# Third column block of an expert's first layer computed at 448 columns ahead of the branch, and the last tile's scaled copy in two halves

## The chip, the cores and the metric

The kernel runs on one core of a Trainium2 chip. A core has five engines with queues of their own: PE (TensorE, matrix products), ACT (ScalarE), DVE (VectorE), POOL (GpSimd) and SP (SyncE, which here only issues transfers). The metric is the device time of one execution in microseconds (us), and the median of the runs counts.

## What is computed

An attention layer with random features is followed by a mixture of experts with 8 experts, on 4 x 576 = 2304 tokens of 512 features. The part that the change touches is the second one:

```python
expert_idx = np.argmax(x @ w_gate, axis=1)              # one expert per token
# disp[e, 0:counts[e]] = rows of x that chose e, at most capacity = 576
h = np.maximum(np.einsum('ecd,edf->ecf', disp, w1), 0.0)     # D 512 -> F 1024
y = np.einsum('ecf,efd->ecd', h, w2)                         # F 1024 -> D 512
out[i] = gate_w[i] * y[expert_idx[i], pos[i]]
```

All inputs are float32. The kernel keeps that precision by splitting each operand into a high and a low part and adding three products: high x high, low x high, high x low.

## The kernel before

**Stages.** The first 165 us or so hold the attention and the routing, which scatters the rows of each expert into a DRAM buffer. Then `opening()` works on the expert that led after the first rows, and a loop takes `e` = 1 to 7. Each expert is one pass: `between(e - 1)` prepares it (transposes its first two tiles of 128 rows, splits the first five blocks of `w1`, finishes the last tile of the expert before, computes the block f = 0 of the first layer at columns 0 to 256), and then `expert(e)` runs.

**Tiles and blocks.** Rows of an expert are columns of the first layer's product: `xh` and `xl` (high and low part) hold up to 576 of them, in tiles of 128. `wide` is 256 columns, `most` is 448. The 1024 hidden features are 8 blocks `f` of 128. `ffn1(f, bank, o, o2, at)` computes block f for the columns o to o2 into PSUM bank `ph` number `bank`, from column `at` on: 4 times L812 (high weights x `xh`) and L813 (low weights x `xh`) in turn, then 4 times L815 (high weights x `xl`), so 12 matmuls. `relu` (L826 on ACT, then L829 on DVE) turns a bank into `h` and its low part.

**Branches.** `expert(e)` asks how many rows the expert has. With over 256 it takes the arm `many`: `prep` transposes tiles 2 and 3 on PE (L745, 4 for each tile), ACT copies each into `xh` (L746) and DVE makes `xl` (L747); PE goes on with f = 1 and f = 2 at 256 columns, for which tiles 0 and 1 suffice. Then a second branch: over 448 rows `to_all`, else `to_most`, which adds the columns 256 to 448 of f = 0, 1 and 2 and does f = 3 to 7 at 448 columns at once. After each `relu`, `behind` splits the next weight block (L117 on ACT, L123 on DVE) and `loads` has SP fetch the next expert's rows and weights (f = 0 and f = 2). Then `later` does the second layer for the tiles 1 to 3; tile 0 is done in the next `between`, or, for the last expert, in the two last lines of the kernel.

**Order.** Each engine takes its instructions in the order in which the code above writes them (a manual schedule), and waits on semaphores where it needs another engine's result. A wait on one engine's semaphore is a count: it covers everything that this engine did up to there.

**The end.** `put` scales a finished tile of the second layer with the gate (`y = py * gt`, L858 on ACT, from a PSUM bank) and has POOL scatter it to the output (L169). For the very last tile `py` is the bank `sm` and `e` is 7.

Of the kernel before, what the change touches and what calls it, by code (L numbers as in the profile page):

```python
# [14 lines left out]
AF = mybir.ActivationFunctionType  # L15
ALU = mybir.AluOpType
# [8 lines left out]
NE, DM, DFF = 8, H * D, 1024  # L25
# [12 lines left out]
def tile_kernel(ctx: ExitStack, tc: tile.TileContext, qT, kT, vT, vv, w_phi, w_g, w1, w2, out, cap):  # L38
    nc = tc.nc
# [128 lines left out]
    def to_out(rows, idx):  # L168
        dma = nc.gpsimd.indirect_dma_start(  # L169
            out=out, out_offset=bass.IndirectOffsetOnAxis(ap=idx.bitcast(U32), axis=0),  # L170
            in_=rows, in_offset=None, bounds_check=NT - 1, oob_is_err=False)
        tc.declare_no_dep(dma.ins, group="outs", reason="distinct rows")
        tc.add_to_no_dep_group("outs", dma.ins)
# [550 lines left out]
    wide = 2 * P  # L724
    most = wide + 3 * D
# [15 lines left out]
    def prep(e, s0, m, pt=None):  # L741
        pt = pt_t[s0 // P % 2] if pt is None else pt
        xh, xl = x2_l[0][:, :, 0], x2_l[0][:, :, 1]
        for k in range(4):
            nc.tensor.transpose(pt[:, k, 0:m], xi_t[e % 2, s0][0:m, k * P:(k + 1) * P], ident[0:m, 0:m])  # L745
        nc.scalar.activation(xh[:, :, s0:s0 + m], pt[:, :, 0:m], AF.Copy)  # L746
        nc.vector.tensor_tensor(xl[:, :, s0:s0 + m], pt[:, :, 0:m], xh[:, :, s0:s0 + m].bitcast(F32),  # L747
                                ALU.subtract)
# [58 lines left out]
    def ffn1(f, bank, o, o2, at=0):  # L807
        hi, lo = w_t[f // 4]
        fs = slice((f % 4) * P, (f % 4 + 1) * P)
        acc = ph_t[bank][:, at:at + o2 - o]  # L810
        for k in range(4):
            nc.tensor.matmul(acc, hi[:, k, fs], xh[:, k, o:o2], start=(k == 0), stop=False)  # L812
            nc.tensor.matmul(acc, lo[:, k, fs], xh[:, k, o:o2], start=False, stop=False)  # L813
        for k in range(4):
            nc.tensor.matmul(acc, hi[:, k, fs], xl[:, k, o:o2], start=False, stop=(k == 3))  # L815
# [8 lines left out]
    def relu(f, bank, o, o2):  # L824
        cuts = sorted({o, o2, *(x for x in [o2 - few(o2)] if o < x < o2)})
        nc.scalar.activation(h_t[f][:, o:o2], ph_t[bank][:, 0:o2 - o], AF.Relu)  # L826
        for a, b in zip(cuts, cuts[1:]):
            at = rest_at(o2, a)
            beat[0] = nc.vector.scalar_tensor_tensor(h_t[f][:, at:at + b - a], ph_t[bank][:, a - o:b - o], 0.0,  # L829
                                           h_t[f][:, a:b].bitcast(F32), ALU.max, ALU.subtract)  # L830
# [18 lines left out]
    def put(e, s0, m, bank):  # L849
        gt, it = gi_t[e % 2, s0]  # L850
        py, y = py_t[bank], y_t[bank % 2]
        if m <= D:
            half = half_t[bank % 2]
            nc.vector.tensor_copy(half[0:m], py[m:2 * m])
            nc.vector.tensor_tensor(half[0:m], half[0:m], py[0:m], ALU.add)
            nc.scalar.activation(y[0:m], half[0:m], AF.Copy, scale=gt[0:m])
        else:
            nc.scalar.activation(y[0:m], py[0:m], AF.Copy, scale=gt[0:m])  # L858
        to_out(y[0:m], it[0:m])


    def between(e):
        t = tiles[0 if e else 2]
        ffn2(wide, *t, 0, range(5))
        prep_gi(e + 1)
        for f in range(2):
            w_split(0, f)
        for x in tiles[:2]:
            prep(e + 1, *x)
        for f in range(2, 5):  # L870
            w_split(f // 4, f % 4)
        ffn2(wide, *t, 0, range(5, 8))
        put(e, *t, 0)
        ffn1(0, 0, 0, wide)
# [8 lines left out]
    def loads(e, f):  # L883
        if f in (0, 2) and e + 1 < NE:
            ask(e + 1, f // 2)

    def later(e, todo, n):
        for i, t in enumerate(todo):
            bank = 3 - i % 2 if len(todo) % 2 else 2 + i % 2
            ffn2(n, *t, bank)  # L890
            put(e, *t, bank)

    def cut(n, t0=1):
        return [(s0, min(m, n - s0)) for s0, m in tiles[t0:] if s0 < n]

    def w2_split(e, *fs):
        for f in fs:
            w_split(2 + f // 4, f % 4)
            if f % 4 == 3 and e + 1 < NE:
                w_load(e + 1, 2 + f // 4)  # L900

    def behind(e, f):
        if f < 3:
            w_split(1, f + 1)
        else:
            w2_split(e, f - 3)

    def to_most(e):
        for f in range(8):
            if f < 3:  # L910
                ffn1(f, f % 4, wide, most, at=wide)
            else:
                ffn1(f, f % 4, 0, most)
            relu(f, f % 4, 0, most)
            behind(e, f)
            loads(e, f)
        w2_split(e, 5, 6, 7)
        later(e, cut(most), most)

    def to_all(e):  # L920
        for f in range(8):
            if f >= 3:
                ffn1(f, f % 4, 0, wide)
            relu(f, f % 4, 0, wide)
            behind(e, f)
            loads(e, f)
            if f == 2:
                for t in tiles[4:]:
                    prep(e, *t)
        w2_split(e, 5, 6, 7)  # L930
        for f in range(8):
            ffn1(f, f % 4, wide, slots)
            relu(f, f % 4, wide, slots)
        later(e, cut(slots), slots)

    def to_two(e):
        for f in range(8):
            if f >= 3:
                ffn1(f, f % 4, 0, wide)
            relu(f, f % 4, 0, wide)  # L940
            behind(e, f)
            loads(e, f)
        w2_split(e, 5, 6, 7)
        later(e, cut(wide), wide)

    def to_one(e):
        for f in range(3):
            relu(f, f % 4, 0, P)
            behind(e, f)
            loads(e, f)  # L950
        for f in range(3, 9):
            if f < 8:
                thin1(f)
                thin_sum(f)
            if f > 3:
                thin_relu(f - 1)
            if f in (4, 6, 7):
                w2_split(e, (f - 3) // 2)
        w2_split(e, *range(3, 8))

    def expert(e):
        with tc.If(cv[e] > wide, label=f"many{e}") as many:
            told(f"most{e}", cv[e] > most)
            for t in tiles[2:4]:
                prep(e, *t)
            for f in range(1, 3):
                ffn1(f, f % 4, 0, wide)
            with tc.If(cv[e] > most, label=f"most{e}") as full:
                to_all(e)
            with full.Else():  # L970
                to_most(e)
        with many.Else():
            told(f"two{e}", cv[e] > P)
            for f in range(1, 3):
                ffn1(f, f % 4, 0, wide)
            with tc.If(cv[e] > P, label=f"two{e}") as two:
                to_two(e)
            with two.Else():
                to_one(e)
# [3 lines left out]
    def told(label, goes):  # L983
        tc.mark_branch_hint_location(label, hint=goes, engines=engines[:3])
# [24 lines left out]
    def opening():  # L1009
# [20 lines left out]
        prep_gi(0, 0, 1)  # L1030
        ffn2(wide, *tiles[0], 1)
        put(0, *tiles[0], 1)
        with tc.If(few_seen > wide - 1, label="seen") as enough:
            ffn2(wide, *tiles[1], 0, range(5))
# [29 lines left out]
    for e in range(NE):  # L1064
        if e:
            if e + 1 < NE:
                count(e + 1)
            expert(e)
        if e == 0:
            nc.vector.tensor_tensor(zi_t, tokf, drop_t, ALU.subtract)  # L1070
        elif e + 1 < NE:
            for b in range(3 * e - 3, 3 * e):
                to_out(fill[:, 0:DM], zi_t[:, b:b + 1])
        if e + 1 < NE:
            told(f"many{e + 1}", cv[e + 1] > wide)
            between(e)
# [35 lines left out]
```

## Time and profile before

| | |
|---|---|
| device time, median of 3 runs (lowest to highest) | 426.77 us (425.67 to 428.6) |
| device time of the profiled execution | 428.85 us |
| its span, first to last instruction | 427.1 us |
| mean granted TensorE clock | 0.989 |
| PE busy / ACT busy / DVE busy | 95% / 58% / 62% |
| passes `e` = 6 and `e` = 7, the two that take `to_most` | from 332.15 to about 374.5, and to about 417 |

All times in a trace are us from the start of the span. A view of the timeline gives each instruction's start and duration; PE's durations overlap, since matmuls are pipelined, so what a matmul costs a busy PE is the distance from start to start. The chain of waits (the chain that ended last) gives that distance directly: each of its pieces is the time that one step added. "<-" names what ended a wait.

### The profile page before, as it was taken

The page shows a single profiled execution, that of the slowest core. Times are in us where ns is not written, and L with a number is a line of the kernel's source. Part 1 is how long each engine was busy: PE and PEld are TensorE (multiplying, and loading weights), DVE is VectorE, ACT ScalarE, POOL GpSimd, SP SyncE. Part 2 cuts the span into 40 slices and gives each one's busy share as a digit, 9 for nine tenths or more (in the row PEclk, how much of TensorE's full clock was granted, in tenths as well). Part 3 has the DMA queues.
Part 4 walks back from the last instruction along what each step waited for, and adds up shares of the span by engine and source line. Part 5 has one row for each costly group of instructions (what it writes and reads, how often), then busy time and mean ns, then how long its engine had stood idle before and what let it go on. Part 6 is the DMA issues. An engine that isn't in the chain of part 4 may idle for free.

```text
span 427.1 us, 12167 instructions
## 1 busy us (share of the span) xinstructions
PE 407.4 (95%) x4813; PEld 358.0 (84%) x4813; DVE 264.7 (62%) x585; ACT 245.9 (58%) x452; POOL 175.1 (41%) x215
## 2 busy tenths in 40 slices
PE   5999999979999999999999999999999999999992
PEld 4778888868898788979979898989898998799871
DVE  5776897858787787744237984757475465156410
ACT  2988687688775586713137865656465454155410
POOL 1758566457576598740035205133250500160011
PEclk9999999998999999999999999999999999999997
DMA  7990599379606653479005996786949266210010
GB/s 250 387 350 5 181 344 357 120 262 296 204 4 214 203 187 122 155 263 363 11 31 171 355 347 213 278 275 176 361 163 331 102 233 216 109 35 1 2 51 29
DMA packets 42715, 82.78 MB, mean 194 GB/s; under 512 B 4351, under 2 KB 9343, under 8 KB 42624
## 3 DMA queue, kind: packets, MB, share of 16 engines
q1 hardware_dynamic: 38080, 72.13, 50.4%
q0 software_dynamic: 4544, 9.47, 6.1%
q8 instruction: 53, 0.87, 0.9%
q14 instruction: 38, 0.31, 0.2%
HBM read 62.65 MB, written 24.30 MB: 204 GB/s over the span
## 4 chain that ended last, share of the span: by engine, by line
PE 91%; DVE 3%; POOL 1%; issue 1%; DMA 1%; ACT 1%; POOLq 0%; SPq 0%; ACTq 0%; DVEq 0%
PE acc L341 10%; PE ph L812 9%; PE ph L813 9%; PE ph L815 9%; PE acc L370 8%; PE pr L259 4%; PE sm L845 4%; PE sm L843 4%; PE sm L846 4%; PE ph L843 4%; PE ph L845 4%; PE ph L846 4%; PE pt L355 4%; PE pr L260 3%; PE pt L745 2%; PE pr L254 1%
## 5 line engine op out<-in xcount | busy, mean ns | idle before, releaser
L169 POOL DMA_INDIRECT out<-y,it x22 | 24.7, 1122 | 165.4 <-ACT y L858 86.8
L123 DVE TENSOR_TENSOR l<-raw,h 128x512 fp32r<-128x512 f32 x118 | 80.1, 710 | 19.7 <-ACT h L117 16.6
L195 POOL TENSOR_TENSOR stk<-px,stk 64x1024 f16<-64x1024 f32 (+1 forms) x30 | 70.9, 2362 | 39.7 <-ACT stk L194 38.8
L812 PE MATMUL ph<-xh,h 128*128 128x256 f32 (+3 forms) x292 | 79.4, 298 | 0.2 <-issue 0.2
L813 PE MATMUL ph<-xh,l 128*128 128x256 f32 (+3 forms) x292 | 78.9, 296 | 0.0
L117 ACT ACTIVATE h<-raw 128x512 fp32r<-128x512 f32 x128 | 75.9, 630 | 0.0
L826 ACT ACTIVATE h<-ph 128x256 fp32r<-128x256 f32 (+3 forms) x67 | 28.8, 430 | 52.9 <-PE ph L815 51.2
L829 DVE SCALAR_TENSOR_TENSOR h<-ph,h 128x256 fp32r<-128x256 f32 (+2 forms) x91 | 33.2, 387 | 38.8 <-ACT h L826 37.9
L812 PEld LDWEIGHTS ph<-xh,h 128*128 128x128 f32 x292 | 55.6, 190 | 1.6 <-issue 0.4
L265 DVE TENSOR_REDUCE m<-pr 128x4 f32<-128x512 f32 x72 | 49.3, 684 | 11.8 <-PE pr L260 7.1
L813 PEld LDWEIGHTS ph<-xh,l 128*128 128x128 f32 x292 | 55.7, 191 | 0.9
L269 DVE TENSOR_TENSOR d<-pr,m 128x512 f32<-128x512 f32 x72 | 49.7, 690 | 3.5
L815 PE MATMUL ph<-xh,h 128*128 128x256 f32 (+3 forms) x292 | 50.9, 296 | 0.0
L341 PE MATMUL acc<-v,kp 128*64 128x73 f32 (+1 forms) x1280 | 47.0, 232 | 1.7 <-issue 1.7
L341 PEld LDWEIGHTS acc<-v,kp 128*64 128x64 f32 (+1 forms) x1280 | 41.2, 138 | 6.6 <-issue 2.7
L370 PE MATMUL acc<-kv,qp 128*64 128x73 f32 x1152 | 44.8, 229 | 0.4 <-issue 0.4
L370 PEld LDWEIGHTS acc<-kv,qp 128*64 128x64 f32 x1152 | 39.3, 136 | 6.5 <-issue 6.2
L815 PEld LDWEIGHTS ph<-xh,h 128*128 128x128 f32 x292 | 42.7, 191 | 0.6
L259 PE MATMUL pr<-whi,stk 128*128 128x128 f16 x260 | 37.0, 222 | 3.3 <-POOL xr L411 3.0
L260 PE MATMUL pr<-wlo,stk 128*128 128x128 f16 x260 | 36.5, 220 | 0.2 <-issue 0.2
L357 ACT ACTIVATE qp<-pt 128x512 f32<-128x512 f32 x36 | 21.5, 597 | 23.9 <-PE pt L355 23.8
L194 ACT ACTIVATE stk<-px 64x1024 f16<-64x1024 f32 (+1 forms) x30 | 34.5, 1150 | 1.0 <-DMA px<-in_kT 0.5
(163 smaller groups left out, 712.5 us busy)
## 6 DMA issues: line engine op xcount, KB each, us to landing
raw<-in_w SPq DMA_DIRECT2D x28, 1024.0 KB, 7.9
xs<-fill SPq DMA_DIRECT2D x18, 514.0 KB, 6.4
xr<-xs SPq DMA_DIRECT2D x24, 257.0 KB, 8.2
raw<-in_w SPq DMA_DIRECT2D x8, 512.0 KB, 3.8
vt<-in_vT SPq DMA_DIRECT2D x3, 1152.0 KB
v<-in_vv SPq DMA_DIRECT2D x2, 1314.0 KB, 7.4
px<-in_kT SPq DMA_DIRECT2D x5, 512.0 KB, 8.9
px<-in_qT SPq DMA_DIRECT2D x4, 640.0 KB, 12.8
```

Source lines behind the costliest of these rows:

```text
L117: nc.scalar.activation(hi, a, AF.Copy)
L123: engine.tensor_tensor(lo, a, hi.bitcast(F32), ALU.subtract)
L195: return lambda: nc.gpsimd.tensor_tensor(t[other], x, t[own], ALU.subtract)
L259: nc.tensor.matmul(pr[:, j], lt, whi, start=True, stop=False)
L260: nc.tensor.matmul(pr[:, j], lt, wlo, start=False, stop=True)
L265: nc.vector.tensor_reduce(m.rearrange("p a b -> p (a b)"), pr, AX.X, ALU.max, apply_absolute_value=True)
L269: beat[0] = nc.vector.tensor_tensor(d, pr, m.to_broadcast([P, 4, NF]), ALU.subtract)
L341: nc.tensor.matmul(acc[f:f + D, a, j * GC:(j + 1) * GC], kp[lo:hi, j, a, f:f + D], vt[lo:hi, r, h * GC:(h + 1) * GC], start=first and j == ...
L370: nc.tensor.matmul(num[lo:hi, g, j * GC:(j + 1) * GC], qp[:, a, j, lo:hi], kv_t[b][:, a, 4 * g + j], start=(a == 0), stop=(a == 1))
L812: nc.tensor.matmul(acc, hi[:, k, fs], xh[:, k, o:o2], start=(k == 0), stop=False)
L813: nc.tensor.matmul(acc, lo[:, k, fs], xh[:, k, o:o2], start=False, stop=False)
L815: nc.tensor.matmul(acc, hi[:, k, fs], xl[:, k, o:o2], start=False, stop=(k == 3))
```

## The change

Two edits. In the arm `many`, f = 2 is computed at 448 columns ahead of the second branch, in place of 256; `to_most` then adds columns 256 to 448 for f = 0 and f = 1 alone. (`to_all`, which starts again from column 256, is written as before; no expert of this input takes it.) In `put`, the last tile of the last expert is scaled in two halves of 256 columns, the first by ACT, the second by DVE.

```diff
-            nc.scalar.activation(y[0:m], py[0:m], AF.Copy, scale=gt[0:m])
+            c = DM // 2 if e == NE - 1 and not s0 else DM
+            nc.scalar.activation(y[0:m, 0:c], py[0:m, 0:c], AF.Copy, scale=gt[0:m])
+            if c < DM:
+                nc.vector.tensor_scalar(y[0:m, c:DM], py[0:m, c:DM], gt[0:m], None, ALU.mult)
         to_out(y[0:m], it[0:m])
...
     def to_most(e):
         for f in range(8):
-            if f < 3:
+            if f < 2:
                 ffn1(f, f % 4, wide, most, at=wide)
-            else:
+            elif f > 2:
                 ffn1(f, f % 4, 0, most)
             relu(f, f % 4, 0, most)
...
             for t in tiles[2:4]:
                 prep(e, *t)
-            for f in range(1, 3):
-                ffn1(f, f % 4, 0, wide)
+            ffn1(1, 1, 0, wide)
+            ffn1(2, 2, 0, most)
             with tc.If(cv[e] > most, label=f"most{e}") as full:
```

PE in the arm `many` of `e` = 7, from the end of f = 1 (bank `ph_3481`) into f = 2 (bank `ph_3482`), before:

```order
L815 MATMUL ph_3481<-xh_2709,h0_2705 128x256 x4
L812 MATMUL ph_3482<-xh_2709,h0_2705 128x256 [waits Activation_49]
L813 MATMUL ph_3482<-xh_2709,l0_2706 128x256 [waits DVE_49]
L812 MATMUL ph_3482<-xh_2709,h0_2705 128x256
L813 MATMUL ph_3482<-xh_2709,l0_2706 128x256
```

The same place and, behind the alternating rows, the end of f = 2 with the branch, of the change (the first and last rows of the block):

```order
L815 MATMUL ph_3481<-xh_2709,h0_2705 128x256 x4
L812 MATMUL ph_3482<-xh_2709,h0_2705 128x448 [waits Activation_49]
L813 MATMUL ph_3482<-xh_2709,l0_2706 128x448 [waits DVE_49]
L812 MATMUL ph_3482<-xh_2709,h0_2705 128x448
L813 MATMUL ph_3482<-xh_2709,l0_2706 128x448
L812 MATMUL ph_3482<-xh_2709,h0_2705 128x448
L813 MATMUL ph_3482<-xh_2709,l0_2706 128x448
L812 MATMUL ph_3482<-xh_2709,h0_2705 128x448
L813 MATMUL ph_3482<-xh_2709,l0_2706 128x448
L815 MATMUL ph_3482<-xh_2709,h0_2705 128x448 [waits DVE_49]
L815 MATMUL ph_3482<-xh_2709,h0_2705 128x448 x3
L971 COMPARE_AND_BRANCH
```

The 12 matmuls of f = 2 now read 448 columns, so tiles 2 and 3 as well; their first one waits for ACT, and the first L815 has a wait for DVE that it did not have.

PE in `to_most` of `e` = 7, where f = 1's second piece ends, before:

```order
L815 MATMUL ph_3481<-xh_2709,h0_2705 128x192 x4
L812 MATMUL ph_3482<-xh_2709,h0_2705 128x192
L813 MATMUL ph_3482<-xh_2709,l0_2706 128x192
L812 MATMUL ph_3482<-xh_2709,h0_2705 128x192
L813 MATMUL ph_3482<-xh_2709,l0_2706 128x192
```

And of the change:

```order
L815 MATMUL ph_3481<-xh_2709,h0_2705 128x192 x4
L812 MATMUL ph_3483<-xh_2709,h0_2705 128x448
L813 MATMUL ph_3483<-xh_2709,l0_2706 128x448
L812 MATMUL ph_3483<-xh_2709,h0_2705 128x448
L813 MATMUL ph_3483<-xh_2709,l0_2706 128x448
```

The 12 matmuls of f = 2's second piece are gone, and f = 3 (bank `ph_3483`) follows f = 1's at once.

DVE at the end of the program, before:

```order
L804 SCALAR_TENSOR_TENSOR h_3447<-sum_3479,h_3447 128x128 [waits Activation_49]
L123 TENSOR_TENSOR l2_3449<-raw_2890,h2_3448 128x512 [waits Activation_49]
L123 TENSOR_TENSOR l3_3451<-raw_3095,h3_3450 128x512 [waits DMAHW4_49,Activation_49]
L123 TENSOR_TENSOR l3_3451<-raw_3095,h3_3450 128x512 [waits Activation_49] x3
L976 UNCONDITIONAL_BRANCH
L1108 UNCONDITIONAL_BRANCH
```

And of the change:

```order
L123 TENSOR_TENSOR l3_3451<-raw_3095,h3_3450 128x512 [waits DMAHW4_49,Activation_49]
L123 TENSOR_TENSOR l3_3451<-raw_3095,h3_3450 128x512 [waits Activation_49] x3
L979 UNCONDITIONAL_BRANCH
L861 TENSOR_SCALAR y_3472<-sm_132,gt_3462 128x256 [waits DMASW1_49,DMASW6_49,DMASW0_49,Activation_49]
L1111 UNCONDITIONAL_BRANCH
```

DVE got one instruction, the second half of the last tile, and this one waits for ACT and not for PE, although PE writes the bank `sm` that it reads.

POOL at the end of the program, before:

```order
L976 ISA [waits DMASW7_49]
L962 ISA [waits DMASW2_49,DMASW1_49,DMASW0_49]
L976 UNCONDITIONAL_BRANCH
L169 DMA out_0<-y_3472,it_3463 2304x512 [waits DMASW3_49,Activation_49,Pool_49]
L1108 UNCONDITIONAL_BRANCH
```

And of the change:

```order
L979 ISA [waits DMASW7_49]
L965 ISA [waits DMASW2_49,DMASW1_49,DMASW0_49]
L979 UNCONDITIONAL_BRANCH
L169 DMA out_0<-y_3472,it_3463 2304x512 [waits DMASW3_49,DVE_49,Pool_49]
L1111 UNCONDITIONAL_BRANCH
```

The last scatter waited for ACT's copy; it now waits for DVE's half, and no longer for ACT by itself.

## Rows read from the trace of the kernel before

**Rows 1.** The page: shares of the span in the chain that ended last.

```profile
PE 91%; DVE 3%; POOL 1%; issue 1%; DMA 1%; ACT 1%; POOLq 0%; SPq 0%; ACTq 0%; DVEq 0%
```

**Rows 2.** Busy time by stretch: length, then PE, PEld, DVE, ACT, POOL, clock, DMA.

```profile
340.27:344.27 4.00, 4.00 (x38) 4.00 (x37) 1.95 (x6) 2.13 (x4) 0.00 (x0) 1.00 0.03 9
344.27:356.46 12.19, 12.19 (x62) 11.30 (x61) 7.00 (x16) 5.32 (x10) 0.00 (x0) 1.00 0.78 268
```

**Rows 3.** Chain in e = 6: start, us added. First L812 of six groups of 12.

```profile
338.83 0.12 PE ph L812
...
340.27 0.09 PE ph L812
...
341.59 0.11 PE ph L812
...
342.93 0.11 PE ph L812
...
346.73 0.20 PE ph L812
...
349.16 0.20 PE ph L812
```

**Rows 4.** Groups by line and shape: count, busy us, mean ns, idle before.

```profile
L812 PE MATMUL ph<-xh,h 128*128 128x256 f32 x196 | 49.6, 285 | 0.2 <-issue 0.2
...
L812 PE MATMUL ph<-xh,h 128*128 128x448 f32 x40 | 14.6, 366 | 0.0
...
L812 PE MATMUL ph<-xh,h 128*128 128x192 f32 x24 | 5.6, 271 | 0.0
```

**Rows 5.** Timeline of e = 6: transposes, ACT's and DVE's copies, f = 2's first matmul.

```profile
336.37 1.03 PE L745 MATMUL pt<-ident,xr 128*128 128x128 f32 x8
...
337.00 1.09 ACT L746 ACTIVATE xh<-pt 128x512 fp32r<-128x512 f32 x2 [1.05 <-PE pt L745]
...
337.63 1.29 DVE L747 TENSOR_TENSOR xh<-pt,xh 128x512 fp32r<-128x512 f32 x2 [1.23 <-ACT xh L746]
...
338.67 0.28 PE L812 MATMUL ph<-xh,h 128*128 128x256 f32 x1
```

**Rows 6.** The same four of e = 7.

```profile
378.69 1.04 PE L745 MATMUL pt<-ident,xr 128*128 128x128 f32 x8
...
380.37 1.09 ACT L746 ACTIVATE xh<-pt 128x512 fp32r<-128x512 f32 x2 [2.10 <-PE pt L745]
...
381.00 0.69 DVE L747 TENSOR_TENSOR xh<-pt,xh 128x512 fp32r<-128x512 f32 x1 [2.27 <-ACT xh L746]
381.00 0.28 PE L812 MATMUL ph<-xh,h 128*128 128x256 f32 x1
```

**Rows 7.** Timeline of e = 6: relu of f = 0, SP's load; then ACT's first split for e = 7.

```profile
341.69 0.55 ACT L826 ACTIVATE h<-ph 128x448 fp32r<-128x448 f32 x1 [3.60 <-PE ph L815]
...
342.32 0.69 DVE L829 SCALAR_TENSOR_TENSOR h<-ph,h 128x384 fp32r<-128x384 f32 x2 [3.40 <-ACT h L826]
...
344.27 2.33 SPq L109 DMA_DIRECT2D raw<-in_w  x2
...
373.31 1.14 ACT L117 ACTIVATE h<-raw 128x512 fp32r<-128x512 f32 x2
```

**Rows 8.** Chain at the end of the program.

```profile
419.00 0.70 ACT y L858
419.69 0.03 POOLq L169
```

**Rows 9.** Groups by line and shape, for the prices of the two halves.

```profile
L829 DVE SCALAR_TENSOR_TENSOR h<-ph,h 128x256 fp32r<-128x256 f32 x48 | 20.3, 423 | 20.4 <-ACT h L826 19.6 <-issue 0.7
L826 ACT ACTIVATE h<-ph 128x256 fp32r<-128x256 f32 x40 | 15.7, 393 | 19.9 <-PE ph L815 19.0 <-PE ph L813 0.9
L826 ACT ACTIVATE h<-ph 128x448 fp32r<-128x448 f32 x16 | 8.7, 546 | 20.9 <-PE ph L815 20.9
L858 ACT ACTIVATE y<-sm,gt 128x512 f32<-128x512 f32 x9 | 6.2, 687 | 5.3 <-PE sm L846 3.3 <-PE ph L812 2.0
```

## The prediction

> **What bounds the kernel now.** I read the page first: a span of 427.1 us, and PE with 91% of the chain that ended last [rows 1]. So a change is worth what it takes from PE's own stream, or adds to it as waiting, plus what lies behind PE's last matmul.
>
> [...]
>
> How often the changed code runs is read from the counts: L812 ran 24 times at 192 columns and 40 times at 448 [rows 4]. A block has 4 of them, and an expert in `to_most` has 3 blocks of 192 and 5 of 448, so 24 / 12 = 40 / 20 = 2 experts, `e` = 6 and 7. A gain per expert counts twice.
>
> **The joined block.** The mean durations (271 and 366 ns, [rows 4]) are no price, since matmuls overlap; by them 12 x (285 + 271 - 366) would give 2.3 us for each expert. The chain gives what a block adds to a busy PE [rows 3]: at 256 columns 340.27 - 338.83 = 1.44 us (f = 2 itself), at 192 columns 342.93 - 341.59 = 1.34, at 448 columns 349.16 - 346.73 = 2.43. Removed: one block of 256 and one of 192 = 1.44 + 1.34 = 2.78 us. Added: one of 448 = 2.43 us. Gain 0.35 us for each expert, 0.70 us for both. In start-to-start steps that is 120, 112 and 203 ns: the 192-column matmul costs nearly as much as the 256-column one, and this is all that the join saves.
>
> [...]
>
> **What the join now waits for.** f = 1 and f = 2 at 256 columns need tiles 0 and 1, and PE works on them while ACT and DVE copy tiles 2 and 3. That cover halves: f = 2 at 448 columns needs ACT's second copy at once, and DVE's second one eight matmuls later.
>
> In `e` = 6 the cover is enough: ACT's two copies run from 337.00 to 338.09, and f = 2 starts at 338.67 [rows 5], 0.58 us later. DVE's end at 338.92, and the first L815 comes 8 x 0.203 = 1.6 us behind the start, at 340.3. No wait.
>
> In `e` = 7 it isn't. PE's transposes start at 378.69 and ACT's copies at 380.37 [rows 6], 1.68 us later, where in `e` = 6 the distance was 337.00 - 336.37 = 0.63 [rows 5]. ACT stood idle for 2.10 us and was released by PE's semaphore, so this lateness of 1.05 us is in the trace, though no work in it explains it. The copies end at 381.46 and f = 2 would start at 381.00: a wait of 0.46 us, or up to 0.58 with a restart as long as one matmul's step (0.12 for the first one of a block, [rows 3]). I take 0.50. DVE's second copy then ends about 382.3 (381.00 + 1.29, the pair of [rows 5]), and the first L815 comes at 381.5 + 1.6 = 383.1. No second wait.
>
> **What is late behind it.** f = 2 now ends 2.43 - 1.44 = 0.99 us later, so f = 0's second piece, its relu (341.69, [rows 7]), the weight splits behind it and SP's loads all start 1.0 us later; everything from f = 3 on starts 0.35 us earlier. ACT's relu of f = 2 then comes at about 345.1 and its split ends at 346.1, ahead of f = 3's relu, which PE lets go at about 346.4 (346.73 - 0.35, [rows 3]). PE's next use of those banks and splits is f = 4 to f = 6, from 346.4 on; f = 0's bank is read out by about 344.0. So this costs nothing while the room is over 2 us; if it were gone, each us of lateness would cost PE a us. SP's weight load of 344.27 [rows 7] goes out at 345.3 and fetches what ACT splits for `e` = 7 from 373.31 on [rows 7]: 28 us of cover. `e` = 7 has no loads of its own.
>
> **The last tile.** Behind PE's last matmul ACT's copy takes 0.70 us of the chain, from 419.00 on, then POOL scatters [rows 8]. Nothing runs beside it, so each ns counts. The order of the change shows DVE's half waiting for ACT and not for PE, and POOL waiting for DVE alone. Both would be wrong unless DVE's wait for ACT stands behind ACT's own half, which in turn waited for PE. So the halves go one after the other. ACT's half: between 0.39 (the relu at 256 columns, 393 ns) and 0.48 (687 less 256 x (546 - 393) / 192 = 204 ns), [rows 9]; I take 0.45, since this copy with its scale is dearer than a relu. The handover: 0.08 (ACT ends at 341.69 + 0.55 = 342.24, DVE starts at 342.32, [rows 7]); 0.03 at the least (a copy that ends at 380.97 by half of the pair, and 381.00, [rows 6]). DVE's half: 0.42 (the relu's low part at 256 columns from the same kind of bank, 423 ns, [rows 9]). Sum 0.45 + 0.08 + 0.42 = 0.95 us for 0.70: a loss of 0.25 us, between 0.14 and 0.28.
>
> **The sum.** -0.70 (two joins) + 0.50 (one wait for ACT) + 0.25 (the tail) = +0.05 us, on the profiled execution's 428.85 us (its span of 427.1 and 1.75 us around it). That execution lies 2.08 us above the median of the three runs; the same difference on the median gives 426.77 + 0.05 = 426.8 us. With the bounds of the unknown prices (wait 0.46 to 0.58, tail 0.14 to 0.28) this case alone reaches from -0.10 to +0.16, so 426.7 to 426.9.
>
> **The rivals.**
>
> *ACT is on time in both experts.* The lateness of 1.05 us has no work behind it in the trace, so it may belong to that one execution. Then f = 2 never waits: -0.70 + 0.25 = -0.45 us, 426.3 us. For it speaks `e` = 6, where the same code was on time; against it, that the rows show the late case in one of two.
>
> *The halves run side by side.* This is what the edit reads like. The tail would take the longer half, 0.45, in place of 0.70: -0.25 in place of +0.25, so in all -0.45 with the wait and -0.95 without, 426.3 or 425.8 us. Against it speaks the order, in which DVE has no wait for PE. [...]
>
> *ACT is late in both experts, slower than before.* If the semaphore that releases ACT comes as late in `e` = 6, its copies end at 338.09 + 1.05 = 339.14 against a start of 338.67: 0.47 to 0.59 us of waiting there too. It decides from 0.58 us of lateness on in `e` = 6, and from none in `e` = 7. Sum: -0.70 + 1.00 + 0.25 = +0.55 us, 427.3 us. Against it speaks that the rows of `e` = 6 show none.
>
> *The join saves nothing in time.* If the distance of a 448-column matmul grew ahead of the branch, where PE has weight loads of the same kind, the gain would go; the five blocks of `to_most` all kept 2.43 us, so I see no reason.
>
> **How the numbers follow.** One late expert 0.45; none late 0.30; both late 0.12; halves side by side 0.08; something not in these rows, over 1% either way, 0.05. The first four lie between -0.95 and +0.55 us, so within 0.25% of the time. About 1% is what a measurement of this kernel can tell from no change, since the three runs alone spread over 0.7%. Faster by over 1% 0.03, within 1% 0.94, slower by over 1% 0.03. The range has to hold a median of runs that themselves lie between 425.67 and 428.6: I shift the ends by the cases (425.67 - 0.95 = 424.7 and 428.6 + 0.55 = 429.2 for a single run, less some 0.3 to 0.6 at each end, since a median scatters less) and take 425.0 to 428.6 us.
>
> **What would show it.** The join: L812 at 192 columns 16 times in place of 24, at 448 columns 48 times in place of 40, at 203 ns from start to start, and f = 0's second piece 0.99 us later behind f = 1 than before. The wait: in each expert, ACT's second copy against f = 2's first matmul; idle PE there, or none. The lateness downstream: PE busy without a gap from f = 0's second piece to the second layer. The tail: DVE's half starting after ACT's half has ended, and POOL released by DVE 0.95 us behind PE's end in place of 0.70. It would be wrong if PE idled behind the branch (the relus late for it), or if the two halves overlapped.

## The result, and the profile after

The changed kernel takes 431.83 us (median of 15 runs) where the kernel before took 427.96 us beside it (15 runs): a ratio of 1.0087 with a 95% interval of 1.0066 to 1.0107, so 3.7 us slower. Forecast were +0.05 us and 426.8 us, with a range that ended at 428.6. The profiled execution of the changed kernel took 430.52 us, with a span of 428.8.

| | before | after |
|---|---|---|
| device time, median, side by side | 427.96 us | 431.83 us |
| profiled execution / its span | 428.85 / 427.1 us | 430.52 / 428.8 us |
| pass `e` = 1 / `e` = 2 | 16.03 / 23.75 us | 17.46 / 25.09 us |
| passes `e` = 3 to `e` = 5 | 23.52, 23.33, 23.33 us | 23.33, 23.33, 23.33 us |
| pass `e` = 6 / `e` = 7 (to PE's end) | 42.32 / 44.52 us | 41.96 / 44.16 us |
| PE's end to the end of the span | 8.28 us | 8.58 us |

A pass is counted from its first transpose on PE to that of the next pass. These lengths are better to compare than whole times: over the profiles of this study pass `e` = 1 began anywhere between 220.4 and 226.5 us, with the same code ahead of it.

The two edits did what the working said. The chain's shares after, the answer to [rows 1]:

```profile
PE 90%; DVE 3%; POOL 1%; issue 1%; DMA 1%; ACT 1%; POOLq 0%; SPq 0%; ACTq 0%
```

The groups by line and shape (count, busy us, mean ns, idle before), the answer to [rows 4] and [rows 9]: 48 and 16 where 40 and 24 stood, and the two halves of the last tile.

```profile
L812 PE MATMUL ph<-xh,h 128*128 128x448 f32 x48 | 17.6, 366 | 0.0
...
L812 PE MATMUL ph<-xh,h 128*128 128x192 f32 x16 | 3.7, 270 | 0.0
...
L861 DVE TENSOR_SCALAR y<-sm,gt 128x256 f32<-128x256 f32 x1 | 0.5, 484 | 4.7 <-ACT y L859 4.7
...
L859 ACT ACTIVATE y<-sm,gt 128x256 f32<-128x256 f32 x1 | 0.5, 474 | 3.3 <-PE sm L846 3.3
```

The chain in `e` = 6 (start, us added), the answer to [rows 3]: f = 2 at 448 columns from 340.95, the two pieces of 192 columns from 343.39 and 344.70, f = 3 from 346.04.

```profile
340.95 0.20 PE ph L812
...
343.39 0.09 PE ph L812
...
344.70 0.11 PE ph L812
...
346.04 0.23 PE ph L812
```

That is 2.44 us for the joined block and 1.31 and 1.34 for the pieces. The end of the program, the answer to [rows 8]: ACT's half, then DVE's, then the scatter.

```profile
420.40 0.48 ACT y L859
420.88 0.02 issue
420.90 0.49 DVE y L861
421.40 0.03 POOLq L169
```

From 420.40 to 421.40 is 1.00 us, for 0.70 before.

**Where the time went.** Busy time by stretch, of the passes `e` = 1, 2, 6 and 7 (length, then PE, PEld, DVE, ACT, POOL, the granted clock, the DMA share, GB/s), before:

```profile
222.03:238.06 16.03, 15.99 (x109) 14.05 (x108) 12.58 (x29) 12.19 (x31) 7.20 (x19) 1.00 0.59 190
238.06:261.81 23.75, 23.57 (x154) 21.40 (x152) 17.24 (x30) 14.74 (x31) 4.15 (x9) 1.00 1.04 342
331.99:374.31 42.32, 42.32 (x238) 37.39 (x236) 18.14 (x37) 17.44 (x32) 7.83 (x17) 1.00 0.45 157
374.31:418.83 44.52, 44.52 (x246) 38.95 (x244) 18.73 (x38) 16.67 (x31) 9.16 (x18) 1.00 0.07 22
```

And after:

```profile
221.57:239.03 17.46, 16.00 (x110) 14.24 (x109) 13.15 (x30) 12.22 (x32) 7.68 (x19) 1.00 0.62 207
239.03:264.12 25.09, 23.72 (x154) 21.46 (x153) 17.18 (x30) 14.66 (x30) 5.02 (x9) 1.00 0.91 307
334.11:376.07 41.96, 41.96 (x226) 36.86 (x224) 18.03 (x37) 17.33 (x32) 7.83 (x17) 1.00 0.46 157
376.07:420.23 44.16, 44.16 (x234) 38.42 (x232) 18.62 (x38) 16.55 (x31) 9.16 (x18) 1.00 0.07 22
```

In `e` = 6 and `e` = 7, where the changed code runs, PE is still busy for all of the stretch, and each is 0.36 us shorter. The loss lies in `e` = 1 and `e` = 2, 1.43 and 1.34 us, with the same instructions on every engine. Their experts have at most 256 rows; they run none of the changed lines. PE simply stands still once in each. The chain at the two places (after):

```profile
233.12 0.06 PE ph L792
233.18 1.25 issue
234.43 0.39 PE ph L790
...
246.25 0.49 PE ph L815 x4
246.75 0.02 issue
246.77 0.39 ACT h L826
247.16 0.53 ACT h L117
247.68 0.38 issue
248.06 0.28 PE ph L812
```

The first is "issue": PE waited for nothing that the profile shows. The second is put down to ACT's relu and weight split of the block just computed, but that is only what happened to run. The weights of the L812 that came late had been loaded before the stop (timeline of the weight loads, after), so the split that they need was done:

```profile
246.45 0.19 PEld L812 LDWEIGHTS ph<-xh,h 128*128 128x128 f32 x1
```

In the kernel before, the next block's L812 at the same place goes on while that relu starts:

```profile
245.90 0.12 PE ph L812
```

```profile
245.94 0.38 ACT L826 ACTIVATE h<-ph 128x256 fp32r<-128x256 f32 x1 [0.54 <-PE ph L815]
```

**What PE lacked.** The page's table of transfers has a queue that carries instructions; that they are PE's is inferred from the times below (queue: packets, MB, share of 16 engines):

```profile
q8 instruction: 55, 0.90, 0.8%
```

0.90 MB in 55 packets is 16 KB a packet. In the packed trace a packet of q8 landed at 233.05, and PE went on at 234.43; another landed at 246.67, and PE went on at 248.06: 1.38 and 1.39 us behind. In the kernel before, PE passed the first of these places at 232.12 without a stop, and there the last packet had landed at 227.79, over 4 us earlier. The change shortens PE's program by 26 instructions for each expert (12 matmuls with their 12 weight loads and two waits), in arms that lie ahead of those that `e` = 1 to `e` = 5 take, so every later arm lies elsewhere against the 16 KB blocks in which code arrives. In PE's compiled program an instruction takes 64 bytes (that of the change is 11,648 bytes shorter, for 7 x 26 = 182 instructions), so 16 KB hold 256. Counted there, with a weight load and its matmul as two, the first stop comes behind instruction 8897 and the second behind 9921. Both counts leave 193 when divided by 256, as they would if a block ended there.

### The profile page after: what moved, and what is told of

It reads as the page before. It is cut to its first block, busy times and chain, and to the rows that moved or that the text cites. A ratio compares the mean times of both kernels' runs of the same rounds, so it can differ in the third digit from the quotient of the medians.

```text
span 428.8 us, 12119 instructions
## 1 busy us (share of the span) xinstructions
PE 406.0 (95%) x4789; PEld 358.5 (84%) x4789; DVE 266.8 (62%) x586; ACT 245.5 (57%) x452; POOL 175.5 (41%) x215
## 4 chain that ended last, share of the span: by engine, by line
PE 90%; DVE 3%; POOL 1%; issue 1%; DMA 1%; ACT 1%; POOLq 0%; SPq 0%; ACTq 0%
PE acc L341 10%; PE ph L812 9%; PE ph L813 9%; PE ph L815 9%; PE acc L370 8%; PE pr L259 4%; PE ph L845 4%; PE ph L843 4%; PE ph L846 4%; PE sm L845 4%; PE sm L846 4%; PE sm L843 4%; PE pt L355 3%; PE pr L260 3%; PE pt L745 2%; PE pr L254 1%
## 5 line engine op out<-in xcount | busy, mean ns | idle before, releaser
L812 PE MATMUL ph<-xh,h 128*128 128x256 f32 (+3 forms) x284 | 78.4, 301 | 1.4 <-ACT h L117 1.3
L813 PE MATMUL ph<-xh,l 128*128 128x256 f32 (+3 forms) x284 | 77.9, 299 | 0.0
L813 PEld LDWEIGHTS ph<-xh,l 128*128 128x128 f32 x284 | 54.1, 190 | 2.4 <-DVE h L829 1.4
L812 PEld LDWEIGHTS ph<-xh,h 128*128 128x128 f32 x284 | 54.1, 190 | 1.3 <-issue 0.2
L815 PE MATMUL ph<-xh,h 128*128 128x256 f32 (+3 forms) x284 | 50.3, 299 | 0.0
L815 PEld LDWEIGHTS ph<-xh,h 128*128 128x128 f32 x284 | 42.1, 191 | 0.7
```

## The experiments

Three theories were tested. **Place** ("layout" in the first expectations): the loss comes from where PE's arms lie against the blocks of code, so it must come without the change and go with padding. **Tail:** it comes from the halves and DVE's new work. **Join:** it comes from f = 2's new place (late relus, splits and loads). A gain or loss in us below is the ratio less 1, times the median of the kernel before in that set (430.07, 429.15 and 429.44 us).

**The join alone.** `put` as before, `to_most` and the arm `many` as in the change (the diff shows the second).

```diff
-            for f in range(1, 3):
-                ffn1(f, f % 4, 0, wide)
+            ffn1(1, 1, 0, wide)
+            ffn1(2, 2, 0, most)
```

> The join alone; the last tile's copy as before. Layout theory (PE's program is 26 instructions shorter for each expert, so every arm behind the first lies elsewhere in the code, and PE waits for code behind taken branches): slower than before by about 3.9 - 0.3 = 3.6 us, though the two passes that run the join (e = 6 and 7) are 0.35 us shorter each. Tail theory (the loss of the change comes with DVE's half): 0.7 us faster than before. Join theory (the joined block itself makes PE wait in e = 6 and 7): slower by about 3.6 us, with those two passes longer.

Measured: ratio 1.0098 (1.0059 to 1.0137), +4.2 us. Passes `e` = 1 and `e` = 2 took 18.86 and 24.73 us, `e` = 6 and `e` = 7 41.96 and 44.97. The whole loss is there without the halves.

**The halves alone.** The join undone.

```diff
-            nc.scalar.activation(y[0:m], py[0:m], AF.Copy, scale=gt[0:m])
+            c = DM // 2 if e == NE - 1 and not s0 else DM
+            nc.scalar.activation(y[0:m, 0:c], py[0:m, 0:c], AF.Copy, scale=gt[0:m])
+            if c < DM:
+                nc.vector.tensor_scalar(y[0:m, c:DM], py[0:m, c:DM], gt[0:m], None, ALU.mult)
```

> The two halves of the last tile alone; the first layer as before. Layout theory and join theory: PE's code is that of before, so only the tail counts, 0.25 to 0.35 us slower (0.1%), not to be told from no change. Tail theory: slower by about 3.6 us.

Measured: ratio 0.9985 (0.9958 to 1.0012), no difference that can be measured. All passes as before (16.03 and 23.70 us in `e` = 1 and `e` = 2), PE's end to the end of the span 8.59 us in place of 8.28. The halves cost 0.30 us and touch no pass.

**The kernel before, with code where the change puts it.** 13 matmuls (26 PE instructions) for each expert are left out of `to_all`, an arm that no expert of this input takes (it would compute wrong values if one did), so everything that runs is the kernel before. Here and below `ffn1` has a parameter `n`, the number of its 12 matmuls that are written.

```diff
-            ffn1(f, f % 4, wide, slots)
+            ffn1(f, f % 4, wide, slots, n=12 - {0: 6, 1: 7}.get(f, 0))
```

> The kernel before, with 13 matmuls for each expert left out of the arm for over 448 rows, which no expert of this input takes (that arm would be wrong if one did). Nothing of what runs differs from before; PE's code is shortened as by the change, so every arm but to_most stands where the change puts it. Layout theory: slower than before by 3.5 to 4.5 us, with no join and no halves. Join theory and tail theory: no difference from before.

Measured: ratio 1.0082 (1.0054 to 1.0109), +3.5 us. Not one executed instruction differs from the kernel before, and the loss is that of the change. This settles place against join and tail. The stop in `e` = 1 is longer in this profile, and it has a second price. Busy time by stretch: up to the stop, the stop, and behind it (columns as above):

```profile
222.45:233.98 11.53, 11.53 (x90) 11.01 (x88) 8.00 (x19) 7.73 (x20) 6.62 (x18) 1.00 0.45 136
233.98:236.60 2.62, 0.01 (x1) 0.00 (x0) 1.16 (x3) 0.64 (x2) 0.26 (x3) 1.00 0.86 306
236.60:238.60 2.00, 2.00 (x7) 1.81 (x8) 0.49 (x2) 0.90 (x4) 0.00 (x0) 0.54 1.07 375
238.60:240.60 2.00, 2.00 (x7) 1.53 (x7) 1.88 (x4) 2.00 (x6) 0.00 (x0) 0.60 0.70 232
240.60:242.21 1.61, 1.61 (x9) 1.25 (x8) 1.61 (x4) 1.61 (x4) 1.05 (x3) 1.00 0.57 85
```

PE stands idle for 2.62 us, and then runs for some 4 us at a granted clock of 0.54 and 0.60 before it is back at 1.00. Pass `e` = 1 is 19.76 - 16.03 = 3.73 us longer: 2.62 of standing still and 1.1 of slow clock. In the profile of the changed kernel the stops were 1.25 and 1.33 us, and the clock stayed at 1.00 in these passes; so that profile shows the mild form. It lost 1.7 us in its span, where the medians lie 3.9 us apart. The length of a stop is no property of its place: behind 8897 PE stood for 1.25 us in the changed kernel, 1.75 in the join alone and 2.62 here, and behind 9921 for 1.33, 1.25 and 0.31, with the same places in all three.

**The change, with PE's code as long as before.** 13 matmuls for each expert are added to the arm that is never taken.

```diff
     def to_all(e):
...
+            if f == 2:
+                ffn1(2, 2, 0, wide, n=1)
+                ffn1(2, 2, 0, wide)
             relu(f, f % 4, 0, wide)
```

> The whole change, and 13 matmuls (26 PE instructions) for each expert put into the arm for over 448 rows, which no expert of this input takes, so that PE's code is as long as before and every arm but one (to_most) stands at the place that it had before. Nothing of what runs differs from the change. Layout theory: the loss goes, and the time is before's -0.7 + 0.3, so 0.4 us faster than before (ratio about 0.999). Join theory and tail theory: as slow as the change, 3.9 us (0.9%) over before.

Measured: ratio 1.0047 (1.0018 to 1.0075), +2.0 us: half of the loss gone. Passes `e` = 1 and `e` = 2 are back at 16.03 and 23.69 us. But the padding stands ahead of `to_most`, and this arm now starts 25 instructions later than in the kernel before, at 14784 of the compiled program, two ahead of a count that leaves 194 (14786). There, right at the jump into the arm, PE stopped, in the chain:

```profile
345.96 1.12 issue
347.08 0.58 PE ph L813 x3
```

So `e` = 6 took 43.37 us in place of 41.96. I had not looked at that arm when I chose the padding. The remedy moved the stop. (An expectation below puts this arm 3 behind a block's start. It counts in a listing that has one branch more for each expert than the compiled program.)

**The join, padded by 11 matmuls, and the change, padded by 11.** With 22 instructions in place of 26, `to_most` starts within 3 instructions of where it did, and the arms of `e` = 1 and `e` = 2 start 4 and 8 earlier.

```diff
+            if f == 2:
+                ffn1(3, 3, 0, wide, n=11)
```

> The join alone (tail as before), with 11 matmuls per expert added in to_all, an arm that no expert of this input takes. PE's code is then 4 instructions per expert shorter than before's, so that to_most starts within 3 instructions of where it started (e = 6 and e = 7), e = 1 starts 4 and e = 2 starts 8 instructions earlier. The place theory (the loss comes from where PE's arms lie against the blocks of 256 instructions in which code is fetched) expects passes e = 1 and e = 2 as before (16.03 and 23.7 us), e = 6 and e = 7 0.36 us shorter each, or e = 7 0.1 us longer if it waits for ACT: -0.7 to -0.2 us against before, ratio 0.998 to 0.9995. A theory that the join itself costs (its later relus, splits and loads), or that any change of the code costs, expects what the join alone cost in the first runs, +3 to +4 us, ratio 1.007 to 1.010.

> The whole change with the same 11 matmuls per expert in the arm that is never taken. The place theory expects the join's -0.7 to -0.2 us plus 0.33 us for the halves at the end (measured in the trace of after): -0.4 to +0.15 us against before, ratio 0.999 to 1.0005, and 0.3 us over the join alone with the same padding. The rival (the join or any change of code costs) expects +3 to +4 us.

Measured: the join 1.0023 (0.9996 to 1.0050), +1.0 us, the change 1.0005 (0.9981 to 1.0030), +0.2 us. The changed kernel's 3.7 us are gone, with the changed code running as it was. The join's expectation (up to 0.9995) lies just below its interval; in its profile the time from the start of `e` = 1 to the end is 0.3 us shorter than in the kernel before, so that profile doesn't show where the +1.0 would lie. Busy time by stretch of the padded change, passes `e` = 1, 2, 6 and 7:

```profile
220.36:236.40 16.04, 16.00 (x109) 14.04 (x108) 12.47 (x29) 12.20 (x31) 7.06 (x19) 1.00 0.68 223
236.40:260.08 23.68, 23.57 (x154) 21.41 (x152) 17.17 (x30) 14.71 (x31) 4.00 (x9) 1.00 0.97 313
330.27:372.23 41.96, 41.96 (x225) 36.86 (x224) 18.02 (x37) 17.32 (x32) 7.83 (x17) 1.00 0.49 165
372.23:417.15 44.92, 44.48 (x234) 38.48 (x232) 18.62 (x38) 16.55 (x31) 9.16 (x18) 1.00 0.07 22
```

`e` = 1, 2 and 6 as the place theory says; `e` = 7 is 0.40 us longer than before, not shorter: the forecast wait for ACT (below). The expectation had `e` = 7 at 0.1 us longer at most, and was 0.3 us too low. The halves' 0.30 us cannot be read from these two ratios; their intervals overlap.

**The change, padded in `e` = 1 and `e` = 2 alone.** The same 13 matmuls under `if f == 2 and e in (1, 2)`.

> The whole change with 13 matmuls added in the never-taken arm of e = 1 and e = 2 alone: their taken arms lie exactly where before has them, while those of e = 3 to e = 7 lie 26 to 105 instructions earlier. If the whole loss is the place of the code in e = 1 and e = 2, as the pass lengths of after say, these two passes are back at 16.03 and 23.7 us, e = 6 and e = 7 keep the 0.36 us each, and the sum is -0.4 us with the halves' 0.33, ratio 0.999 (up to 1.0005 if e = 7 waits for ACT). If the later arms' places matter as well, or the loss belongs to the change and not to the place, it stays over +1 us.

Measured: ratio 1.0028 (0.9993 to 1.0063), +1.2 us with an interval that holds both nothing and 2.7. The passes tell more: 16.04 and 23.69 in `e` = 1 and `e` = 2, 41.96 and 44.92 in `e` = 6 and `e` = 7. From the start of `e` = 1 to the end of the span it is 0.1 us longer than the kernel before, so what the ratio has beyond that isn't in its profile.

**The kernel before, moved by a whole block.** 128 matmuls, 256 PE instructions, are added for each expert to the arm never taken.

```diff
+            if f == 2:
+                for _ in range(10):
+                    ffn1(3, 3, 0, wide)
+                ffn1(3, 3, 0, wide, n=8)
```

> Before, with 128 matmuls = 256 PE instructions for each expert added in to_all, the arm that is never taken: every arm behind it lies elsewhere in memory, but at the same place within its block of 256 instructions. The place theory, if what counts is the place within a block, expects no difference: within 0.3% of before, passes e = 1 and e = 2 at 16.03 and 23.7 us. A theory that longer jumps or any shift of the code cost expects +2 us or more, above all in e = 1 and e = 2.

Measured: ratio 1.0001 (0.9971 to 1.0031); passes 16.02 and 23.71 us. Ten times the change's shift, and 1792 instructions of it by `e` = 7, cost nothing that can be measured: neither the length of the jumps nor the size of the program counts here, but the place within 256 instructions.

**The kernel before, moved by other amounts.** As in the kernel with 13 matmuls less: 4 less, 8 less, 26 less, and 13 more.

> Before with 4 matmuls (8 PE instructions) per expert left out of to_all, the arm that no expert of this input takes, so that e = 1's taken arm starts 19 instructions ahead of the end of a 256-instruction block in place of 11 (in the padded kernels 7 and 15 ahead cost nothing, 37 ahead cost 1.3 to 2.6 us), and e = 2's 15 ahead. A theory in which the distance to the block's end counts smoothly expects little, 0 to 0.5 us in the passes e = 1 and e = 2 together; a theory that only a return to the old places is free expects 2 us or more.

> Before with 8 matmuls (16 PE instructions) per expert left out of the arm never taken: e = 1's arm starts 27, e = 2's 31 instructions ahead of a block's end. By the distance, between the free cases (up to 15) and the costly one (37, 1.3 to 2.6 us in e = 1): 0.5 to 1.5 us in e = 1, and some in e = 2 (which at 51 ahead cost 0.3 to 1.3). Ratio 1.000 to 1.006.

> Before with 26 matmuls (52 PE instructions) per expert left out of the arm never taken, twice the change's shift: e = 1's arm starts 63 instructions ahead of a block's end, e = 2's 103 ahead. If the loss grows with the shift, e = 1 and e = 2 cost over 4 us. If it is the place within the block, the passes e = 3 to e = 5 of after (63 to 91 ahead, no loss) say that both may be nearly free: 0 to 1 us, ratio 1.000 to 1.003.

> Before with 13 matmuls (26 PE instructions) per expert added to the arm never taken: the same size of shift as the change's, the other way. e = 1's arm starts 15 instructions behind a block's start, e = 2's 52 behind. A theory that any shift costs expects the change's +3 us; by place, an arm that starts just behind a block's start has the whole block ahead of it (as e = 2 in before, 1 behind: no idle PE), so 0 to 0.7 us, unless the start itself comes late as in to_most of e = 6 in the padded change (1.1 us idle at its start, 3 behind a block's start).

| kernel before, PE instructions per expert moved by | ratio (95% interval) | in us | `e` = 1 | `e` = 2 | other pass |
|---|---|---|---|---|---|
| -8 | 1.0090 (1.0056 to 1.0125) | +3.9 | | | |
| -16 | 1.0161 (1.0122 to 1.0200) | +6.9 | 20.64 | 24.74 | |
| -26 | 1.0082 (1.0054 to 1.0109) | +3.5 | 19.76 | 23.79 | |
| -52 | 0.9986 (0.9960 to 1.0011) | -0.6 | 16.02 | 23.59 | |
| +26 | 1.0053 (1.0024 to 1.0082) | +2.3 | 16.02 | 23.62 | `e` = 5: 27.27 |
| +256 | 1.0001 (0.9971 to 1.0031) | 0.0 | 16.02 | 23.71 | |

(No passes are given for -8: its profiled execution took 438.34 us, 1% more than the median of its runs.)

So place decides: the loss doesn't grow with the shift, and twice the change's shift is free. My rule for the size was wrong, though. From the distance between an arm's start and the end of its block I expected at most 0.5 us for -8, 0.5 to 1.5 us and some more for -16, and at most 0.7 for +26; they cost 3.9, 6.9 and 2.3. For -16 PE stopped three times; the two stretches are those of `e` = 1 and `e` = 2:

```profile
220.70:241.34 20.64, 17.32 (x109) 15.66 (x108) 13.79 (x31) 12.96 (x33) 8.41 (x21) 0.92 0.59 182
241.34:266.08 24.74, 23.59 (x153) 21.40 (x152) 16.64 (x29) 14.15 (x29) 4.26 (x8) 1.00 0.92 308
```

The stops are 1.07 us behind instruction 8641, 2.25 behind 8897 and 1.16 behind 9921, all counts that leave 193 once more, with a clock of 0.92 over `e` = 1. For +26 a stop of 2.19 us came in `e` = 5, right at a taken branch (to 13925, in the midst of a block). So the stops here came in two forms: behind a count that leaves 193, and at a jump (2.19 us here, 1.12 in `to_most` of the first padding). Which boundary or jump stalls, of the many that PE passes without a gap, these runs don't settle. The kernel also marks each branch with a hint (`told`) some way ahead of it; no run changed or left out the hints, so their part in this is open.

## Why the prediction was wrong

**The join's price: right.** A pass with the join and without a wait is 0.36 us shorter, in both experts, where 0.35 was worked out from starts in the chain.

**The wait for ACT: right in its mechanism, too small in its size, and absent where first looked for.** In `e` = 6 there is none, in any of the six kernels with the join (in the one with 13 matmuls of padding for every expert, the stop in `to_most` is PE's only one). In `e` = 7 ACT's copies came late in thirteen of the fourteen profiles, 1.66 to 1.82 us behind PE's first transpose, where `e` = 6 always had 0.63 or 0.64. The one exception is the changed kernel's own profile: transposes at 380.44, copies at 381.08, 0.64 behind, f = 2 without a wait (timeline, answers [rows 6]).

```profile
380.44 1.04 PE L745 MATMUL pt<-ident,xr 128*128 128x128 f32 x8
381.08 1.09 ACT L746 ACTIVATE xh<-pt 128x512 fp32r<-128x512 f32 x2 [1.06 <-PE pt L745]
```

The other five profiles with the join have the wait. In the join alone:

```profile
382.74 1.04 PE L745 MATMUL pt<-ident,xr 128*128 128x128 f32 x8
...
384.56 1.08 ACT L746 ACTIVATE xh<-pt 128x512 fp32r<-128x512 f32 x2 [2.24 <-PE pt L745]
...
385.70 0.47 PE L812 MATMUL ph<-xh,h 128*128 128x448 f32 x1 [0.49 <-ACT xh L746]
```

The first matmul of the joined block starts 2.96 us behind the first transpose, where it would have at 2.31: 0.65 us. The next one comes 0.31 behind it, in place of 0.20. So the wait costs 0.76 us, as the passes say (44.92 with it, 44.16 without), not 0.50: the copies were 0.13 us later than in [rows 6], a handover of 0.04 and the slow first matmul were left out. It takes back both joins: -0.72 + 0.76 = +0.04 us. The chances of 0.45 for one late expert and 0.30 for none should have been further apart. What makes ACT late there is open. The prediction read [rows 6] as a release by PE, but by the packed trace of the kernel before the four transposes of the first copy had ended at 379.29, and ACT started 1.08 us behind them; in the changed kernel's profile it started 0.03 us behind them. Whether ACT lacked instructions there, as the packets of q8 suggest for PE at its stops, isn't shown.

**The lateness behind the join: right.** From the branch on PE is busy for 5.09 of 5.09 and 12.16 of 12.16 us (after, `e` = 6, answers [rows 2]):

```profile
340.95:346.04 5.09, 5.09 (x38) 4.91 (x37) 0.70 (x4) 1.06 (x2) 0.00 (x0) 1.00 0.16 56
346.04:358.20 12.16, 12.16 (x62) 11.27 (x61) 8.22 (x20) 6.27 (x12) 0.00 (x0) 1.00 0.78 269
```

The relus, splits and loads that come 1.0 us later cost nothing.

**The last tile: right in its order, a little too small in its size.** The halves went in turn: 0.48, 0.02 and 0.49, with the scatter behind DVE. Against 0.45 + 0.08 + 0.42, the copy with its scale was dearer than a relu and the handover cheaper. The loss is 0.30 us where 0.25 was said, just outside 0.14 to 0.28.

**The sum: wrong, by the term that wasn't in it.** Its own terms with what they measured, -0.72 + 0.76 + 0.30 = +0.34 us, would have given no difference that can be measured, and the padded change (+0.2 us, with an interval from -0.8 to +1.3) agrees with that. The step that failed is the first: that the change is worth what it takes from PE's stream in the experts that run it, so in two passes of seven. Left out was that it shortens PE's program by 26 instructions for each expert, ahead of the arms that the others take. I looked at the order of the instructions that run and not at where they lie. It is a cost that no rival named: 2.8 us in two passes of the profile after, 3.8 in that of the join alone (18.86 + 24.73 - 16.03 - 23.75), 3.8 with the code of before in the places of the change (19.76 + 23.79 - 16.03 - 23.75). The 0.05 for something outside the rows was the only room that it had, and the range left it out.

From the start of `e` = 1 to the end of the span, where the profiles can be compared, the passes account for most of the ratios: +3.7 us for the join alone (measured +4.2), +3.6 for the short code of before (+3.5), +2.0 for the first padding (+2.0), +5.8 for -16 (+6.9), +0.3 for the padded change (+0.2), -0.4 for -52 (-0.6). For the changed kernel itself it is +2.2 against +3.7: its profile has the shorter stops and no wait for ACT in `e` = 7 (0.76 us). For +26 it is +3.6 against +2.3, and its profiled execution (434.61 us) lies above the median (432.10).

No version here beats the kernel before by what can be measured. The join in `e` = 6 alone, with code at the places of before, would by the passes be worth 0.36 us, under a tenth of a per cent; it was not tried.

## What to carry to other kernels

Here an edit that took 26 PE instructions for each expert out of the program moved all the code behind it, and two passes whose own instructions stayed as they were took 2.8 us longer, where the two joins were worth 0.72; so compare the passes that an edit doesn't run before explaining those that it does. To price such an edit, run it a second time with its code's length restored in an arm that is never taken, and look whether the padding moves another arm (here 13 matmuls of it brought a stop of 1.12 us into `to_most`). And count the restart with the wait: here the second matmul behind a wait came 0.31 us behind the first in place of 0.20, and behind the stops of 1.75 us and more the granted clock was 0.50 to 0.70.

## What was not expected of the hardware

- The instructions on q8 come in packets of 16 KB. In the passes `e` = 1 to `e` = 7 of these profiles (that of -8 left out) PE stood idle without a wait for another engine eleven times, for 0.31 to 2.62 us (less than 0.3 us is not counted), and each time it went on 1.3 to 1.6 us after a packet had landed.
- Where that happened went with the place within 256 instructions: moved by 256 the kernel took the same time (1.0001), moved 16 earlier it was 1.6% slower, 52 earlier it was not (0.9986). Nine of the eleven stops come behind a count that leaves 193 when divided by 256, the other two at a jump.
- Stops of 0.31 to 1.33 us left the granted clock at 1.00. Behind one of 1.75 us it was 0.51 and 0.66 in the two stretches of 2 us that followed (the join alone), behind one of 2.25 us 0.70 and 0.50 (-16), behind one of 2.62 us 0.54 and 0.60. Behind one of 2.19 us it was 0.62 and 0.60 (kernel of before moved by +26, the stop and the two stretches behind it):

```profile
314.94:317.13 2.19, 0.00 (x0) 0.01 (x1) 1.11 (x2) 0.90 (x2) 2.03 (x10) 1.00 0.07 14
317.13:319.50 2.37, 2.37 (x13) 2.37 (x14) 0.00 (x0) 0.00 (x0) 0.38 (x1) 0.62 0.97 306
319.50:321.50 2.00, 2.00 (x13) 2.00 (x13) 1.12 (x2) 0.91 (x2) 0.00 (x0) 0.60 0.90 336
```
